# Joining six pairs of neighbouring loads in a two-layer decode kernel that streams all its data through one buffer

## The chip, the cores and the metric

The kernel runs on one core of a Trainium2 chip. The metric is the device time of one execution in microseconds (us); lower is better. A difference is spoken of as a share of the time of the kernel before.

## What is computed

Two layers of a decoder for one new token of four sequences (B = 4, D = 512). Each layer is an attention with a cache (32 query heads, 8 heads of keys and values, 4096 cached positions, 128 numbers each), and then a gated feed-forward network (F = 1792). Both layers use the same weights and the same cache. Everything is float32.

```python
x = A_x
x = x + A(_layernorm(x), k_cache, v_cache, wq, wo)
x = x + B(_layernorm(x), w1, w3, w2)
x = x + A(_layernorm(x), k_cache, v_cache, wq, wo)
x = x + B(_layernorm(x), w1, w3, w2)

# A: q = x @ wq; p = softmax(q k / sqrt(128)); (p @ v) @ wo
# B: (silu(x @ w1) * (x @ w3)) @ w2
```

## The kernel before

**One array, one buffer.** The host lays weights and cache side by side in one array `rows` of 128 partitions, in the order in which layer 0 uses them. On the chip there is one buffer, `space`, of 218 slots; a slot is 256 numbers in each of 128 partitions, 128 KB. All reading from memory is a list of loads, `LOADS`, one DMA each, written out by hand. An entry `(src, n, at)` copies n slots from slot `src` of the array into the buffer from slot `at` on. Two entries named "stash" are no DMAs but copies from PSUM by ScalarE.

**When a load is issued.** `pump` (line 120) goes through the list in its order and never past an entry whose slots are not all free:

```python
            if any(taken[at:at + n]):
                return
            taken[at:at + n] = [True] * n
            ...
                nc.sync.dma_start(place(at, n), rows[:, lo:lo + n * KB])
```

`done` (line 149) gives slots back after the last use in program order, and calls `pump`. So the list fixes where each DMA stands in the program. On the chip SyncE (SP) issues the DMAs (line 140) in this order; each first waits until the engine that last read its slots is through. The DMAs take eight semaphores in turn, and before a semaphore is used again SP waits for the load that used it last. The waits of SP stand in its queue: a load that waits holds up every load behind it.

**Who waits for a load.** A consumer waits for the whole DMA that holds its piece, since a DMA has one semaphore.

**Attention.** Keys and values of a head come as 32 tiles of 4 slots: tiles 0 to 15 are keys, 16 to 31 values, and each kind is in two halves of 8 tiles (the halves `c` of the cache). `score` (line 311, matmuls at L322) multiplies the query with 8 tiles of keys. `maximum`, `exponent` (ScalarE, L341) and `turn` (TensorE transposes at L348, and the VectorE copy at L350) make the weights. `weigh` (line 381, matmuls at L387) multiplies these with 8 tiles of values. For one head TensorE runs: score, turn, score, `weigh` of the first half, `turn` of the second half's weights, `weigh` of the second half. TensorE works through its queue in order.

**Where the layers meet.** Layer 0 takes the heads 0 to 7, layer 1 takes them from 7 down to 0, so that head 7 stays in the buffer. Its keys of tiles 0 and 1 must make room, though: they are copied into PSUM and brought back later (the stash). The last of these four copies is `store_last` (line 392): ScalarE copies half of tile 1 into the PSUM buffer of `turn`, once VectorE has copied the turned weights out of it (`finish`, line 398, calls `turn`, then `store_last`, then the second `weigh`). Only after it are the slots of tile 1 (158 to 162) free. The next load in the list, w3's first part `(1180, 16, 146)`, goes into slots 146 to 162, and so it waits for that copy at L395. Behind it in the list come w1 and the rest of w3 and w2, for the feed-forward of layer 0 (`feed_forward`, line 454: L463 for w1 and w3, L503 for w2), then the head 7 values that were given up, then head 6 for layer 1.

Of the kernel before, what the change touches and what calls it, by code (L numbers as in the profile page):

```python
# [52 lines left out]
    (0, 32, 186), (32, 64, 54), (96, 64, 118), (160, 64, 0), (224, 64, 91), (288, 64, 24), (352, 48, 88),  # L53
    (400, 48, 136), (448, 64, 28), (512, 60, 92), (572, 64, 152), (636, 52, 92), (688, 32, 144), (720, 40, 178),
    (1120, 32, 60), (760, 64, 113), (824, 40, 177), (864, 28, 92), (892, 36, 120), (928, 32, 174), (960, 32, 92),
    (992, 32, 154), (1024, 32, 186), (1056, 16, 0), (1072, 16, 92), (1088, 16, 108), (1104, 8, 124), (1112, 8, 132),
    (1180, 16, 146), (1152, 8, 0), (1160, 8, 8), (1168, 12, 16), (1196, 6, 140), (1202, 6, 146), (1208, 4, 158),
    (1212, 4, 152), (1216, 2, 156), (1218, 4, 140), (1222, 2, 144), (1224, 4, 146), (1228, 2, 150), (1230, 2, 158),
    (1232, 2, 160), (1234, 2, 152), (1056, 4, 154), (1060, 4, 140), (1064, 4, 144), (1068, 4, 148), (864, 4, 158),
    (868, 8, 68), (876, 4, 186), (880, 4, 190), (884, 8, 194), ("stash", 1, 202), (892, 8, 206), ("stash", 0, 214),  # L60
    (900, 8, 84), (908, 12, 162), (920, 12, 174), (932, 32, 108), (964, 20, 140), (984, 8, 36), (736, 28, 190),
    (764, 36, 84), (800, 64, 120), (608, 64, 52), (160, 32, 116), (672, 64, 154), (480, 64, 52), (544, 36, 148),
    (580, 28, 190), (320, 64, 28), (8, 24, 92), (384, 64, 154), (192, 64, 28), (256, 64, 140), (32, 32, 28),
    (64, 32, 60), (96, 32, 104), (128, 16, 136), (144, 8, 39), (152, 8, 28), (0, 8, 210), (1180, 16, 164),
    (1196, 12, 95), (1208, 8, 108), (1216, 8, 58), (1224, 4, 214), (1228, 4, 210), (1232, 2, 0), (1234, 2, 182),
)
# [580 lines left out]
```

## Time and profile before

| | us |
|---|---|
| median of 3 runs | 704.14 |
| lowest and highest | 703.93, 704.21 |
| the profiled execution, whole | 704.12 |
| its span, first to last instruction | 702.3 |
| TensorE busy in the span | 421.3 |
| VectorE busy | 144.5 |
| ScalarE busy | 41.7 |

The whole time is 1.8 us longer than the span; this lies ahead of the first instruction and behind the last. Views of the trace that are used below: the page of the profile (shares of engines and DMA queues, and the chain of waits that ended last), the chain by time (each step with start and length in us, a DMA from its issue to its landing), the timeline (start, length, engine, line, and in brackets the idle time ahead and what ended it), the DMA issues (KB, and us from issue to landing), and sums over stretches (busy time of each engine, granted TensorE clock, DMA share, GB/s). SPq is SyncE's queue; a count such as x16 in a matmul row takes in the weight loads, so it is 8 matmuls.

### The profile page before, as it was taken

Reading aid. Unit: us, or ns where it says so; the run is one execution under the profiler, and the core shown is the slowest. Engines: PE = TensorE matmul, PEld = TensorE weight load, DVE = VectorE, ACT = ScalarE, POOL = GpSimd, SP = SyncE. Lnnn points to the kernel's source line nnn. Section 1 sums busy time; section 2 is a strip of 40 time slices with the busy share of each in tenths; the row PEclk is TensorE's granted clock in tenths of the full one; section 3 lists DMA queues with packets and bytes.
Section 4 is the critical chain, followed back from the end, with each engine's and each line's share of the span. In section 5 each row is a group of like instructions: output and inputs, shape, how many; then the busy total and the mean of one; then the engine's idle time right before and its main releaser. Section 6 shows DMA issues by size and latency. Waiting matters only on the chain.

```text
span 702.3 us, 7502 instructions
## 1 busy us (share of the span) xinstructions
PE 421.3 (60%) x3280; PEld 133.4 (19%) x3280; DVE 144.5 (21%) x512; ACT 41.7 (6%) x100; POOL 3.1 (0%) x10
## 2 busy tenths in 40 slices
PE   1265466644578409667688985744555734567576
PEld 0111121201112103121124221201111211121223
DVE  2012112121023103330231322112120301213221
ACT  0010000100001001000101210000100001000100
POOL 0000000000000000000000000000000000000000
PEclk9997677876769859886999997877877958779999
DMA  9999999999999999999999999999999999999996
GB/s 422 418 415 425 467 419 418 426 457 417 449 414 444 424 438 415 436 423 427 422 418 378 423 430 440 439 438 418 441 440 414 450 419 448 430 425 417 424 425 268
DMA packets 12991, 297.87 MB, mean 424 GB/s; under 512 B 1440, under 2 KB 1568, under 8 KB 4512
## 3 DMA queue, kind: packets, MB, share of 16 engines
q1 hardware_dynamic: 12960, 297.41, 99.0%
q8 instruction: 25, 0.41, 0.2%
q14 instruction: 6, 0.05, 0.0%
HBM read 297.34 MB, written 0.07 MB: 423 GB/s over the span
## 4 chain that ended last, share of the span: by engine, by line
DMA 71%; PE 24%; DVE 1%; another core or an unknown queue 1%; ACT 1%; issue 1%; SPq 0%; ACTq 0%; DVEq 0%
DMA space<-in_rows 71%; PE o L387 10%; PE scores L322 9%; PE sums_ps L306 1%; PE turned L348 1%; ACT p L341 1%; PE scores L202 1%; PE stored L251 1%; DVE acc L335 0%; DVE pT L350 0%; PE o L463 0%; SPq L140 0%; PE sums_ps L431 0%; PE sums_ps L420 0%
## 5 line engine op out<-in xcount | busy, mean ns | idle before, releaser
L322 PE MATMUL scores<-space,qT 128*32 128x512 f32 x1024 | 170.0, 713 | 141.6 <-DMA space<-in_rows 140.8
L387 PE MATMUL o<-space,pT 128*16 128x512 f32 x1024 | 152.8, 710 | 99.3 <-DMA space<-in_rows 91.5
L322 PEld LDWEIGHTS scores<-space,qT 128*32 128x32 f32 x1024 | 36.0, 123 | 218.6 <-issue 180.0
L387 PEld LDWEIGHTS o<-space,pT 128*16 128x16 f32 x1024 | 31.7, 108 | 198.3 <-issue 94.2
L335 DVE TENSOR_REDUCE acc<-scores 128x1 f32<-128x512 f32 x32 | 22.1, 691 | 181.5 <-PE scores L322 181.5
L341 ACT ACTIVATE p<-scores,acc 128x512 f32<-128x512 f32 x30 | 20.6, 687 | 559.0 <-DVE acc L335 432.1
L410 DVE SCALAR_TENSOR_TENSOR o<-o,acc,o 128x128 f32<-128x128 f32 x112 | 39.3, 351 | 49.2 <-PE o L387 45.8
L350 DVE COPY pT<-turned 128x256 f32<-128x256 f32 x32 | 13.6, 425 | 154.3 <-PE turned L348 154.3
L348 PE MATMUL turned<-ident,p 128*128 128x128 f32 x128 | 21.9, 296 | 11.8 <-ACT p L341 11.8
L295 PE MATMUL sums_ps<-space,xT 128*32 128x512 f32 x120 | 22.9, 704 | 2.4 <-DMA space<-in_rows 2.4
L421 DVE COPY o<-sums_ps 128x16 f32<-128x16 f32 x16 | 2.8, 175 | 98.1 <-PE sums_ps L420 98.1
L348 PEld LDWEIGHTS turned<-ident,p 128*128 128x128 f32 x128 | 14.0, 145 | 44.1 <-ACT p L341 25.7
L306 PEld LDWEIGHTS sums_ps<-same,shares 128*128 128x128 f32 x120 | 16.3, 211 | 16.8 <-DVE shares L301 11.1
L306 PE MATMUL sums_ps<-same,shares 128*128 128x4 f32 x120 | 17.6, 270 | 0.9 <-DVE shares L301 0.9
L463 PE MATMUL o<-space,xT 128*32 128x192 f32 (+1 forms) x256 | 13.7, 355 | 3.2 <-DMA space<-in_rows 1.5
L441 PE MATMUL stored<-space,o 128*32 128x512 f32 x104 | 13.5, 592 | 0.0
L301 DVE TENSOR_SCALAR shares<-sums_ps,columns 128x512 f32<-128x512 f32 x15 | 11.1, 743 | 1.7 <-PE sums_ps L295 1.7
L503 PE MATMUL sums_ps<-space,hT 128*4 128x128 f32 x224 | 9.1, 272 | 3.6 <-DMA space<-in_rows 2.9
L211 PE MATMUL o<-columns,same 128*32 128x1 f32 x64 | 2.0, 181 | 14.3 <-DVE columns L548 13.3
L420 PEld LDWEIGHTS sums_ps<-columns,o 128*128 128x128 f32 x32 | 6.1, 239 | 20.6 <-issue 13.0
L463 PEld LDWEIGHTS o<-space,xT 128*32 128x32 f32 x256 | 7.6, 110 | 8.4 <-DVE h L480 2.8
L420 PE MATMUL sums_ps<-columns,o 128*128 128x16 f32 x32 | 7.7, 318 | 0.6 <-DVE o L410 0.6
(101 smaller groups left out, 141.9 us busy)
## 6 DMA issues: line engine op xcount, KB each, us to landing
space<-in_rows SPq DMA_DIRECT2D x11, 4096.0 KB, 21.6
space<-in_rows SPq DMA_DIRECT2D x14, 1024.0 KB, 18.6
space<-in_rows SPq DMA_DIRECT2D x3, 4608.0 KB, 24.6
space<-in_rows SPq DMA_DIRECT2D x2, 6144.0 KB, 30.9
space<-in_rows SPq DMA_DIRECT2D x6, 2048.0 KB, 29.2
space<-in_rows SPq DMA_DIRECT2D x3, 3584.0 KB, 23.5
space<-in_rows SPq DMA_DIRECT2D x2, 5120.0 KB, 28.7
space<-in_rows SPq DMA_DIRECT2D x1, 7680.0 KB, 33.8
```

The lines of the kernel that those rows point to most:

```text
L295: nc.tensor.matmul(wide[32 * k:32 * k + 32, :], xT[:, 32 * k:32 * k + 32], w[:, k, :], start=True, stop=True)
L306: nc.tensor.matmul(misc[:, h * B:(h + 1) * B], shares[:, h * DH:(h + 1) * DH], same[:, 0:B], start=True, stop=True)
L322: nc.tensor.matmul(ps[32 * b:32 * b + 32, :], qT[:, b, at:at + 32], t[:, i * BLOCK:(i + 1) * BLOCK], start=(m < 2), stop=(m >= TILES - 2))
L335: nc.vector.tensor_reduce(acc[:, i:i + 1], ps, axis=AX.X, op=ALU.max, negate=True)
L341: nc.scalar.activation(p.rearrange("p n s -> p (n s)"), ps, AF.Exp, bias=acc[:, i:i + 1], scale=1.0 if scale is None else scale, accum_out ...
L348: nc.tensor.transpose(pt[:, n, :], p[:, n, :], ident)
L350: nc.vector.tensor_copy(pT, pt.rearrange("p n (b r) -> p n b r", b=B)[:, :, :, 0:ROW])
L387: nc.tensor.matmul(o_ps[i][32 * b:32 * b + ROW, :], pT[:, r // 2, b, :], t[:, j * NB * DH:(j + 1) * NB * DH], start=(r < 2), stop=(r >= TI ...
L410: nc.vector.scalar_tensor_tensor(o, o_ps[s][:, j * DH:(j + 1) * DH], acc[:, 16 + NB * s + j:17 + NB * s + j], o, op0=ALU.mult, op1=ALU.add)
L420: nc.tensor.matmul(misc[:, 0:B * REP], o, head, start=True, stop=True)
L441: nc.tensor.matmul(bank[32 * h:32 * h + 32, :], oT[:, h, :], w[:, h, :], start=first, stop=last)
L463: nc.tensor.matmul(bank[32 * j:32 * j + 32, s], xT[:, 32 * k:32 * k + 32], w[:, j], start=(k == 0), stop=(k == KC - 1))
```

## The change

Six times two neighbouring entries of `LOADS` become one entry. Nothing else in the file is changed. The order of the list stays, and there are six DMAs fewer, of the same bytes.

| join | before | after | what it holds |
|---|---|---|---|
| 1 | (1072, 16, 92), (1088, 16, 108) | (1072, 32, 92) | layer 0, head 7: value tiles 20 to 23 and 24 to 27 |
| 2 | (1152, 8, 0), (1160, 8, 8) | (1152, 16, 0) | layer 0: first columns of w1, chunks 0, 1 and 2, 3 |
| 3 | (1230, 2, 158), (1232, 2, 160) | (1230, 4, 158) | layer 0: w2 chunks 11 and 12 |
| 4 | (876, 4, 186), (880, 4, 190) | (876, 8, 186) | layer 1, head 6: key tiles 3 and 4 |
| 5 | (908, 12, 162), (920, 12, 174) | (908, 24, 162) | layer 1, head 6: key tiles 11 to 13, and 14, 15 with value tile 16 |
| 6 | (544, 36, 148), (580, 28, 190) | (544, 64, 148) | layer 1, head 3: value tiles 16 to 24, and 25 to 31, which move from slots 190 to 218 into 184 to 212 |

```diff
...
-    (992, 32, 154), (1024, 32, 186), (1056, 16, 0), (1072, 16, 92), (1088, 16, 108), (1104, 8, 124), (1112, 8, 132),
+    (992, 32, 154), (1024, 32, 186), (1056, 16, 0), (1072, 32, 92), (1104, 8, 124), (1112, 8, 132),
...
```

The table is two lines shorter, so line numbers below it are smaller by 2 in the kernel after. SP's queue of the kernel before, from the load (1056, 16, 0) to w3's second part; 128x4096 is 16 slots or 2048 KB, DMAHW is the semaphore of an earlier load, PE and Activation are TensorE and ScalarE as last readers:

```order
L140 DMA space<-in_rows 128x4096
L140 DMA space<-in_rows 128x4096 [waits DMAHW4_49,PE_49]
L140 DMA space<-in_rows 128x4096 [waits PE_49]
L140 DMA space<-in_rows 128x2048 x2
L140 DMA space<-in_rows 128x4096 [waits DMAHW5_49,Activation_49]
L140 DMA space<-in_rows 128x2048 [waits DMAHW7_49,PE_49]
L140 DMA space<-in_rows 128x2048 [waits DMAHW6_49,PE_49]
L140 DMA space<-in_rows 128x3072
L140 DMA space<-in_rows 128x1536 [waits DMAHW0_49]
```

The same place after the change:

```order
L138 DMA space<-in_rows 128x4096
L138 DMA space<-in_rows 128x8192 [waits DMAHW4_49,PE_49]
L138 DMA space<-in_rows 128x2048 x2
L138 DMA space<-in_rows 128x4096 [waits DMAHW5_49,Activation_49]
L138 DMA space<-in_rows 128x4096 [waits DMAHW7_49,PE_49]
L138 DMA space<-in_rows 128x3072
L138 DMA space<-in_rows 128x1536 [waits DMAHW6_49]
```

Join 1 makes one 128x8192 of two 128x4096, join 2 one 128x4096 of two 128x2048. The load that waits for ScalarE (Activation) stands where it stood, two loads of 128x2048 behind join 1.

TensorE's queue of the kernel before, from the value tiles 20 to 23 of head 7 on (o_94 is the result of the first `weigh`, o_95 that of the second):

```order
L387 MATMUL o_94<-space,pT 16x512 [waits DMAHW0_49]
L387 MATMUL o_94<-space,pT 16x512 x7
L348 MATMUL turned<-ident,p 128x128 [waits Activation_49]
L348 MATMUL turned<-ident,p 128x128 x3
L387 MATMUL o_95<-space,pT 16x512 [waits DMAHW1_49,DVE_49]
L387 MATMUL o_95<-space,pT 16x512 x7
L387 MATMUL o_95<-space,pT 16x512 [waits DMAHW2_49]
```

After the change:

```order
L385 MATMUL o_94<-space,pT 16x512 [waits DMAHW0_49]
L385 MATMUL o_94<-space,pT 16x512 x7
L346 MATMUL turned<-ident,p 128x128 [waits Activation_49]
L346 MATMUL turned<-ident,p 128x128 x3
L385 MATMUL o_95<-space,pT 16x512 [waits DVE_49]
L385 MATMUL o_95<-space,pT 16x512 x7
L385 MATMUL o_95<-space,pT 16x512 [waits DMAHW1_49]
```

The order of the matmuls is the same. The first row now waits for the joined load, which stands ahead of the transposes; the first matmul of o_95 has no wait for a load any more.

More of the change, by code (lines that the diff above doesn't have):

```diff
@@ L55 @@
     (1120, 32, 60), (760, 64, 113), (824, 40, 177), (864, 28, 92), (892, 36, 120), (928, 32, 174), (960, 32, 92),
[4 rows of a table removed]
-    (868, 8, 68), (876, 4, 186), (880, 4, 190), (884, 8, 194), ("stash", 1, 202), (892, 8, 206), ("stash", 0, 214),
[3 rows of a table removed]
[3 rows of a table added]
+    (868, 8, 68), (876, 8, 186), (884, 8, 194), ("stash", 1, 202), (892, 8, 206), ("stash", 0, 214),
[2 rows of a table added]
     (64, 32, 60), (96, 32, 104), (128, 16, 136), (144, 8, 39), (152, 8, 28), (0, 8, 210), (1180, 16, 164),
```

10 rows, old and new, of the table LOADS are left out of this document.

## The prediction

> **What bounds the kernel now.** I read the page first: how full each engine and the DMA queue are, and which chain ended last.
>
> ```profile
> span 702.3 us, 7502 instructions
> DMA  9999999999999999999999999999999999999996
> q1 hardware_dynamic: 12960, 297.41, 99.0%
> DMA 71%; PE 24%; DVE 1%; another core or an unknown queue 1%; ACT 1%; issue 1%; SPq 0%; ACTq 0%; DVEq 0%
> ```
>
> The queue that carries the loads is busy for 99.0% of the span, and no slice but the last is under nine tenths. So the DMA engines are the bound, and hardly anything else counts: a change gains only by making the 297.41 MB cheaper to move, and loses whenever it lets the queue run dry, since nothing makes up for that later. The sums over three stretches show where bytes are dear.
>
> ```profile
> 40.00:340.00 300.00, 179.02 (x1186) 53.13 (x1186) 59.95 (x203) 14.96 (x40) 0.00 (x0) 0.78 1.00 430
> 340.00:400.00 60.00, 47.28 (x558) 18.71 (x559) 14.77 (x58) 9.94 (x21) 1.26 (x2) 0.94 1.01 406
> 400.00:690.00 290.00, 176.75 (x1317) 53.65 (x1316) 62.01 (x223) 15.09 (x38) 0.55 (x1) 0.81 1.00 431
> ```
>
> The last column is GB/s. Where the layers meet (340 to 400 us) it is 406 instead of 430, at a DMA share of 1.0: busy, but on smaller loads. At full rate these bytes would take 60 x 406 / 430.5 = 56.6 us, so 3.4 us are lost there. Some 31 loads land in it, so a load costs at most 3.4 / 31 = 0.11 us beyond its bytes.
>
> **What a load costs.** The chain by time gives landings to a hundredth.
>
> ```profile
> 364.62 10.62 DMA space<-in_rows
> ...
> 376.24 5.59 DMA space<-in_rows
> ```
> ```profile
> 472.69 23.07 DMA space<-in_rows
> ...
> 503.03 31.46 DMA space<-in_rows
> ```
>
> The lower two are landings at 495.76 and 534.49; by the list two loads of 64 slots (16.78 MB) came between them, in 38.73 us: 433.2 GB/s. The upper two are landings at 375.24 and 381.83; by the list eight loads of 2 or 4 slots with 2.62 MB came between, in 6.59 us. At 433.2 GB/s the bytes would take 6.05, so eight loads cost 0.54 us: 0.07 each. Six loads fewer gain 6 x 0.07 = **0.4 us**; by the stretch above 0.7 at most, and nothing at least. I take 0.4, from the row of the small loads themselves.
>
> In the Trainium skill, "DMA: Bandwidth & Descriptors", section "Anatomy of one DMA", a DMA has a fixed cost of about 2.0 us, and "Rules for kernel authors" there says to join many small transfers into one. If each of the six paid that on the path, the estimate would be 12 us, or 692; the rows above have 0.07 in place of 2.0, since in a full queue the next load moves while the last one completes.
>
> **What a joined load delays.** It can be issued only when both places are free, so its first half is issued later; and it lands once, so its first half is there later. The first costs something only if the queue ahead runs short. Here are the second loads of the pairs, in the order of the joins, each with its time from issue to landing:
>
> ```profile
> space<-in_rows SPq DMA_DIRECT2D x1, 2048.0 KB, 27.9
> ...
> space<-in_rows SPq DMA_DIRECT2D x1, 1024.0 KB, 13.8
> ...
> space<-in_rows SPq DMA_DIRECT2D x1, 256.0 KB, 5.5
> ...
> space<-in_rows SPq DMA_DIRECT2D x1, 512.0 KB, 7.5
> ...
> space<-in_rows SPq DMA_DIRECT2D x1, 1536.0 KB, 12.8
> ...
> space<-in_rows SPq DMA_DIRECT2D x1, 3584.0 KB, 28.3
> ```
>
> Their own bytes take 4.8, 2.4, 0.6, 1.2, 3.6 and 8.5 us at 433.2 GB/s; the rest, 4.9 us for join 3 and 6 to 23 for the others, is work queued ahead. So when each joined load is issued, at the time of its second half, the queue still has 4.9 us or more. An empty queue needs at most 2.4 us to move again (below). The later issue costs nothing at any of the six.
>
> The later landing holds up TensorE. For join 3 that is by 0.6 us at most, in front of a queue of 4.9 us: nothing. Joins 2, 4 and 5 had their second halves issued, and were first used, at these times:
>
> ```profile
> 351.49 0.38 SPq L140 DMA_DIRECT2D space<-in_rows  x1
> ...
> 386.05 0.38 SPq L140 DMA_DIRECT2D space<-in_rows  x1
> ...
> 395.75 0.33 SPq L140 DMA_DIRECT2D space<-in_rows  x1
> ```
> ```profile
> 365.17 1.07 PE L463 MATMUL o<-space,xT 128*32 128x256 f32 x16
> ...
> 404.55 1.90 PE L322 MATMUL scores<-space,qT 128*32 128x512 f32 x16
> ...
> 411.76 1.91 PE L322 MATMUL scores<-space,qT 128*32 128x512 f32 x12
> ```
>
> The second halves landed at 351.49 + 13.8 = 365.3, 386.05 + 7.5 = 393.6 and 395.75 + 12.8 = 408.6: 0.1 us after the first use for join 2, ahead of it for the others. Join 6 puts off the first `weigh` of head 3 by the 8.5 us of its second half at most; what waits for the end of that head is a load of 64 slots:
>
> ```profile
> 558.06 41.85 DMA space<-in_rows
> ```
>
> Issued 8.5 us later it would have 33 us to its landing, of which its own bytes take 19.4: nothing again. If these covers were thinner than the rows say, each would cost what join 1 does.
>
> **Join 1 is the costly one.** What stands on the way from its first half to the next load, in the timeline:
>
> ```profile
> 340.61 1.91 PE L387 MATMUL o<-space,pT 128*16 128x512 f32 x16 [0.86 <-DMA space<-in_rows]
> ...
> 345.50 3.39 PE L387 MATMUL o<-space,pT 128*16 128x512 f32 x16 [2.98 <-DMA space<-in_rows]
> ...
> 348.82 0.66 PE L348 MATMUL turned<-ident,p 128*128 128x128 f32 x4
> ...
> 349.51 0.42 DVE L350 COPY pT<-turned 128x256 f32<-128x256 f32 x1 [8.14 <-PE turned L348]
> ...
> 349.97 0.60 ACT L395 ACTIVATE turned<-space 128x512 f32<-128x512 f32 x1 [8.27 <-DVE pT L350]
> ...
> 350.51 1.91 PE L387 MATMUL o<-space,pT 128*16 128x512 f32 x16 [1.04 <-DVE rows L356]
> ...
> 350.60 1.85 SPq L140 DMA_DIRECT2D space<-in_rows  x4
> ```
>
> Tiles 20 to 23 land, TensorE starts on them at 345.50, transposes, VectorE copies, ScalarE makes its last stash copy, and at 350.60 SP issues w3's first part, 5.10 us after TensorE's start. That SP waited for this copy and nothing later:
>
> ```profile
> SPq L140 <- ACT turned L395: 24.6, 1, 24.6
> ```
>
> Behind it on SP all of w1, w3 and w2 are queued. Ahead of it in the DMA queue are the two 1024 KB loads behind join 1, and how long those last is in the chain by time; the waiting load's own row follows.
>
> ```profile
> 323.28 32.04 DMA space<-in_rows
> ```
> ```profile
> space<-in_rows SPq DMA_DIRECT2D x1, 2048.0 KB, 9.7
> ```
>
> The second of them lands at 355.32, and w3's part at 350.60 + 9.7 = 360.3, one load later: no pause, with 4.7 us in hand. After the change tiles 20 to 23 are there only when 24 to 27 are: issued at 322.44, 27.9 us to landing, so at 350.3 instead of 345.5. If all runs on as before, w3 is issued at 350.3 + 5.1 = 355.4, when the last load ahead of it has just landed. The queue is empty, and every load for the feed-forward stands behind this one.
>
> The 5.10 us depend on TensorE's clock. The 8 matmuls at 345.50 took 3.39 us, those at 350.51 took 1.91; the sums over these stretches have the clock in the column ahead of the DMA share.
>
> ```profile
> 345.50:348.40 2.90, 2.90 (x16) 0.48 (x16) 0.00 (x0) 0.00 (x0) 0.00 (x0) 0.50 0.93 393
> 348.60:351.80 3.20, 2.16 (x21) 0.83 (x20) 2.05 (x12) 1.81 (x2) 0.00 (x0) 1.00 1.04 422
> ```
>
> After 2.98 us of idling the clock was 0.50; after the change TensorE idles from 342.5 to 350.3, so I take 0.50 again. At full clock the issue would be 1.48 us earlier, at 353.9. At half clock for the transposes as well it would be 0.46 later, at 355.9; the price of these at half clock is in another place:
>
> ```profile
> 198.99 1.12 PE L348 MATMUL turned<-ident,p 128*128 128x128 f32 x4
> ```
>
> The Trainium skill, "TensorE: Matmul & The Clock Gate", Part 1, says that the clock falls to half after an idle window of about 3.4 us and needs a busy one of that length to rise; by it the half clock is certain here and may last through the transposes, which is the sum with 355.4 to 355.9.
>
> What an empty queue costs the trace shows only at its two ends: the first load, and the store of the output.
>
> ```profile
> space<-in_rows SPq DMA_DIRECT2D x1, 4160.0 KB, 12.2
> ...
> out<-space SPq DMA_DIRECT2D x1, 64.0 KB, 1.5
> ```
>
> The first: 4.26 MB take 9.8 us at 433.2 GB/s, so 2.4 us go to starting and landing. The second: 0.15 us of bytes, so 1.35. The first is the nearer, a load into an idle queue. w3's 2.10 MB take 4.8 us, so it lands at 355.4 + 2.4 + 4.8 = 362.6 instead of 360.3: **2.3 us late**. The ends: 2.8 (issue at 355.9), 1.3 (1.35 in place of 2.4), 0.8 (issue at 353.9) and 0 (both).
>
> TensorE's own delay I cost at nothing: it starts the second `weigh` some 0.6 us ahead of the new issue, at 354.8 in place of 350.51, but no longer waits within it for the two 1024 KB loads, which are there by then. So it comes out of the attention late by no more than some 2 to 4 us, and what it needs next, w3, is late by 2.3 too; the slots that it frees after that shift with the loads. If that cover is gone, the rest of these 4 us comes on top.
>
> **The sum.** Against the profiled execution's own 704.12 us, 0.02 under the median of the runs: -0.4 + 2.3 = +1.9, or **706.0 us**. From -0.7 (no pause) to +2.8 (nothing gained).
>
> **The rivals.**
>
> *The pause is short.* TensorE's clock comes back early, or a queue in the middle of the program starts faster than the first load did. Loss 0 to 1.3, net -0.4 to +0.9: about 704.4. For it: the store's 1.35. Against it: a TensorE that idles for 7.8 us.
>
> *No pause at all.* The w3 load is issued before 352.9, 2.4 us ahead of the end of the queue; the chain from landing to issue would have to take 2.6 us in place of 5.10. Then only the gain is left: 703.7, not slower. This is also what comes out if the joined half's landing isn't what the first `weigh` waits for. Against it speaks TensorE's queue, whose first row there waits for the joined load.
>
> *The short loads are the loss.* All 3.4 us lost between 340 and 400 go away with deeper loads, in spite of the pause: 704.12 - 3.4 + 2.3 = 703.0; faster. Against it: 25 of the 31 loads remain. If a load cost what the empty queue shows, 6 x 2.4 = 14 us would go and the time be 690; that the eight loads took 6.59 us speaks against it. This second one is the skill's fixed cost.
>
> *A second pause.* One of the later joins also drains the queue: 2 us more, 708.0. Against it: 4.9 us or more ahead of each.
>
> **How the numbers follow.** A measurement of this kernel can tell about 0.2%, 1.4 us, from no change. The forecast (pause of 1.3 to 2.8 us) has 0.66; of this 0.58 is beyond 1.4 us after the gain, 0.08 within. The short pause has 0.20 (same), no pause 0.07 (same), the dear loads 0.04 together (faster), the second pause 0.03 (slower). So faster 0.04, same 0.35, slower 0.61. The range takes in no pause and the longest pause with nothing gained, and a little beyond: 703.7 to 707.2.
>
> **What would show it.** In the trace after: w3's issue near 355.4 instead of 350.6, still behind ScalarE's copy (L393 there); the 1024 KB load ahead of it lands near 355.3; w3 lands about 7.2 us after its issue; a stretch between 355 and 358 with far fewer GB/s; everything behind late by some 2 us and no more. I am wrong if the issue is before 353, if GB/s shows no hole there, or if the later loads catch up.

## The result, and the profile after

The kernel after takes 708.19 us (median of 6 runs, 707.28 to 708.71) against 704.18 of the kernel before beside it (703.93 to 704.76): a ratio of 1.0055, with a 95% interval of 1.0042 to 1.0068. It is slower by 4.0 us. The forecast was 706.0, and its range ended at 707.2: the direction was right, the size half of what it is. The profiled execution took 707.70 us, 3.6 more than that of the kernel before.

The page of the kernel after, the same parts as were shown of before:

```profile
span 705.9 us, 7490 instructions
DMA  9999999999999999999989999999999999999996
q1 hardware_dynamic: 12096, 297.41, 98.4%
DMA 70%; PE 26%; DVE 2%; another core or an unknown queue 1%; ACT 1%; issue 1%; SPq 0%; ACTq 0%; DVEq 0%
```

There are fewer packets for the same 297.41 MB. The queue is busy for 98.4% of a longer span instead of 99.0%, and one slice, the 21st, has fallen from 9 to 8. The sums over the three stretches of the kernel after (the last columns are granted clock, DMA share and GB/s):

```profile
40.00:340.00 300.00, 178.28 (x1186) 53.15 (x1186) 59.96 (x203) 14.60 (x38) 0.00 (x0) 0.78 1.00 431
340.00:400.00 60.00, 41.30 (x525) 17.89 (x529) 13.12 (x51) 8.83 (x18) 1.25 (x2) 0.94 0.94 379
400.00:690.00 290.00, 180.26 (x1284) 52.40 (x1280) 62.97 (x229) 15.54 (x40) 0.11 (x1) 0.81 1.00 431
```

The outer two are as before. Where the layers meet, the DMA share is 0.94 instead of 1.01 and the rate 379 GB/s instead of 406. So the loss arose there. The timeline of the kernel after at that place:

```profile
340.63 1.91 PE L385 MATMUL o<-space,pT 128*16 128x512 f32 x16 [0.91 <-DMA space<-in_rows]
...
350.47 3.62 PE L385 MATMUL o<-space,pT 128*16 128x512 f32 x16 [7.93 <-DMA space<-in_rows]
354.02 0.66 PE L346 MATMUL turned<-ident,p 128*128 128x128 f32 x4
354.72 0.42 DVE L348 COPY pT<-turned 128x256 f32<-128x256 f32 x1 [13.37 <-PE turned L346]
...
355.17 0.60 ACT L393 ACTIVATE turned<-space 128x512 f32<-128x512 f32 x1 [13.50 <-DVE pT L348]
355.20 3.63 PE L385 MATMUL o<-space,pT 128*16 128x512 f32 x32 [0.52 <-DVE pT L348]
...
355.80 10.32 SPq L138 DMA_DIRECT2D space<-in_rows  x6
```

This is the chain that the prediction foresaw, step by step: TensorE idles 7.93 us for the joined load instead of 2.98, works at half clock on tiles 20 to 23, and ScalarE's last stash copy ends at 355.77 instead of 350.57. SP still waits for this copy last and issues w3 at 355.80 instead of 350.60:

```profile
SPq L138 <- ACT turned L393: 29.8, 1, 29.8
```

The DMA issues give from issue to landing, for w3's first load (issued at 355.80) and the joined w1 load behind it:

```profile
space<-in_rows SPq DMA_DIRECT2D x1, 2048.0 KB, 7.4
...
space<-in_rows SPq DMA_DIRECT2D x1, 2048.0 KB, 12.9
```

w3 lands at 363.2, 2.9 us later than the 360.3 of before. Now the sums over short stretches, first of the kernel after:

```profile
350.00:353.00 3.00, 2.53 (x12) 0.49 (x16) 0.00 (x0) 0.00 (x0) 0.00 (x0) 0.50 0.82 341
353.00:355.00 2.00, 1.68 (x12) 0.42 (x4) 0.28 (x1) 0.00 (x0) 0.00 (x0) 0.73 0.15 61
355.00:358.00 3.00, 2.80 (x28) 0.83 (x32) 2.69 (x14) 2.09 (x3) 0.00 (x0) 1.00 0.47 109
358.00:361.00 3.00, 2.42 (x14) 0.82 (x6) 1.61 (x6) 0.00 (x0) 0.00 (x0) 1.00 0.97 415
```

The hole is deeper than the late landing says, and it begins earlier. The last load ahead of w3 landed at 355.35, yet from 353 to 355 us the DMA share is already 0.15. The share is a mean over 16 DMA engines (a transfer's whole time counts where it starts). The trace records sixteen completions of each load. Of this last load, seven came from 352.01 to 352.86, seven more from 353.68 to 353.96, and the last two at 355.26 and 355.35: most engines were through well ahead of the landing, which is the last completion. The idle DMA time is 3 x 0.18 + 2 x 0.85 + 3 x 0.53 = 3.8 us. With the forecast gain of 0.4 us for six loads fewer, that is 3.4 us net, where the profiled executions differ by 3.6.

The same records show what the pause did to the engines' order. In the kernel before, the completions of w3's first load are spread from 357.35 to 360.25; in the kernel after, from 362.52 to 363.22. The last of them is 2.97 us late, but on the mean of the sixteen they are 4.4 us late.

So at this point there were two ways to count the loss. **Theory 1**, the prediction's: it is the lateness of w3, the pause of the last DMA engine (2.9 us here). **Theory 2**: it is the idle time of all 16 together (3.8 us), since the engines that were ahead lose their head start in the pause. Two rivals blame something else: **rival A**, that one of the other five joins costs about 1 us as well; **rival B**, that the size of the joined load costs, not its lateness.

### The profile page after: what moved, and what is told of

It reads as the page before. It is cut to its first block, busy times and chain, and to the rows that moved or that the text cites. A ratio compares the mean times of both kernels' runs of the same rounds, so it can differ in the third digit from the quotient of the medians.

```text
span 705.9 us, 7490 instructions
## 1 busy us (share of the span) xinstructions
PE 421.1 (60%) x3280; PEld 133.6 (19%) x3280; DVE 144.5 (20%) x512; ACT 41.7 (6%) x100; POOL 3.0 (0%) x10
## 3 DMA queue, kind: packets, MB, share of 16 engines
q1 hardware_dynamic: 12096, 297.41, 98.4%
## 4 chain that ended last, share of the span: by engine, by line
DMA 70%; PE 26%; DVE 2%; another core or an unknown queue 1%; ACT 1%; issue 1%; SPq 0%; ACTq 0%; DVEq 0%
DMA space<-in_rows 70%; PE scores L320 11%; PE o L385 8%; PE sums_ps L304 1%; PE turned L346 1%; ACT p L339 1%; DVE acc L333 1%; PE stored L249 1%; DVE o L408 0%; PE sums_ps L293 0%; PE o L461 0%; PE stored L439 0%; PE sums_ps L501 0%; DVE pT L348 0%
## 5 line engine op out<-in xcount | busy, mean ns | idle before, releaser
L385 PE MATMUL o<-space,pT 128*16 128x512 f32 x1024 | 149.3, 700 | 100.5 <-DMA space<-in_rows 93.2
L346 PE MATMUL turned<-ident,p 128*128 128x128 f32 x128 | 23.6, 313 | 11.3 <-ACT p L339 11.2
```

The lines of the kernel that those rows point to most:

```text
L346: nc.tensor.transpose(pt[:, n, :], p[:, n, :], ident)
L385: nc.tensor.matmul(o_ps[i][32 * b:32 * b + ROW, :], pT[:, r // 2, b, :], t[:, j * NB * DH:(j + 1) * NB * DH], start=(r < 2), stop=(r >= TI ...
```

## The experiments

For each, "350 to 358" is a row of sums of its profile; what its DMA share lacks to that of before, times 8 us, is the idle DMA time. The row of the kernel before, and that of the kernel after:

```profile
350.00:358.00 8.00, 5.59 (x33) 1.20 (x34) 3.20 (x15) 2.06 (x3) 0.00 (x0) 0.83 1.01 419
```
```profile
350.00:358.00 8.00, 7.01 (x48) 1.74 (x52) 2.97 (x14) 2.09 (x3) 0.00 (x0) 0.75 0.52 184
```

8 x (1.01 - 0.52) = 3.9 us by this coarser row. Intervals are those of the ratio to the kernel before, run beside each.

**Five joins without the first.** In the kernel after:

```diff
-    (1072, 32, 92),
+    (1072, 16, 92), (1088, 16, 108),
```

> Joins 2 to 6 alone, join 1 undone. Theory (all of the 4.0 us is join 1: it holds back the copy for which w3's load waits, and the DMA queue runs dry): 703.8 us, 0.35 under the kernel before (5 loads x 0.07 us), no hole in the queue between 355 and 358 us. Rival A (one of the later joins costs about 1 us as well): 705 us or more.

Measured: 703.96 us, ratio 0.9993 (0.9982 to 1.0003). The row of 350 to 358:

```profile
350.00:358.00 8.00, 5.09 (x35) 1.00 (x35) 3.95 (x16) 2.00 (x3) 0.00 (x0) 1.00 1.03 419
```

No hole, and no slower than the kernel before. Rival A falls. The gain of five loads fewer, 0.2 us, is within what can be told from nothing.

**Join 1 alone.** In the kernel before:

```diff
-    (1072, 16, 92), (1088, 16, 108),
+    (1072, 32, 92),
```

> Join 1 alone. Theory: 708.5 us, the kernel after plus five loads at 0.07 us; w3's first load is issued near 355.8 us and lands near 363.2. Rival A (a later join costs 1 us): 707.2 us or less.

Measured: 707.78 us, ratio 1.0050 (1.0037 to 1.0063): the whole loss within its interval. w3 is issued at 356.42 in its profile, 0.6 us later than forecast, mainly since here the four transposes ran at half clock too (1.11 us).

```profile
350.00:358.00 8.00, 6.84 (x32) 1.70 (x36) 2.38 (x13) 2.09 (x3) 0.00 (x0) 0.50 0.47 169
```

**The two halves apart, but in the other order.** In the kernel before:

```diff
-    (1072, 16, 92), (1088, 16, 108),
+    (1088, 16, 108), (1072, 16, 92),
```

> The kernel before with the two halves of join 1 left apart but loaded in the other order, so that value tiles 20 to 23 land second, at 350.4 us, as they do in the joined load; as many loads as before, of the same sizes. Theory (what counts is when these tiles are there): 708.5 us, w3 issued near 355.8. Rival B (the size of the joined load, or its single DMA, is what costs): 704.2 us.

Measured: 707.92 us, ratio 1.0050 (1.0038 to 1.0062). The timeline shows the same wait without any joined load, and the same half clock:

```profile
350.57 3.62 PE L387 MATMUL o<-space,pT 128*16 128x512 f32 x16 [7.89 <-DMA space<-in_rows]
...
355.52 0.60 ACT L395 ACTIVATE turned<-space 128x512 f32<-128x512 f32 x1 [13.71 <-DVE pT L350]
...
356.14 0.80 SPq L140 DMA_DIRECT2D space<-in_rows  x2
```
```profile
350.00:358.00 8.00, 6.92 (x44) 1.87 (x48) 2.66 (x13) 2.09 (x3) 0.00 (x0) 0.71 0.48 175
```

Rival B falls: what costs is when tiles 20 to 23 are there, not how many DMAs bring them.

**All six joins, with work put ahead of the wait.** In the kernel after, w3's first load is cut; chunks 0 to 2 need no slot of tile 1:

```diff
-    (1180, 16, 146),
+    (1180, 12, 146), (1192, 4, 158),
```

> All six joins, but w3's first load cut in two: chunks 0 to 2 (1536 KB, slots 146 to 158), which need not wait for the last stash copy, and chunk 3 (512 KB, slots 158 to 162), which does. Theory: the first part is in the queue early and gives it 3.6 us of work beyond 355.3, the second is issued near 355.8 with some 3 us in hand, so there is no pause: 703.8 to 704.2 us. Rival A: 705 us. If TensorE's own delay of 1.5 to 4 us at this place costs time by itself: 705.5 us or more.

Measured: 705.33 us, ratio 1.0028 (1.0009 to 1.0046). Its row:

```profile
350.00:358.00 8.00, 6.96 (x44) 1.93 (x48) 2.50 (x13) 2.09 (x3) 0.00 (x0) 0.66 0.87 344
```

This missed: by the medians more than half of the loss is gone, but 1.2 us are left, though the queue had 3.6 us more to do and w3's last part landed at 360.4, hardly later than before. The single executions range from 704.03 to 710.98, four of the twelve at 707.98 or more, so the interval is wide (0.6 to 3.2 us). Theory 1 has no place for the 1.2 us; the DMA share does: 8 x (1.01 - 0.87) = 1.1 us. It could also have been TensorE's own delay; the last two runs below bear on that.

**A smaller delay.** In the kernel before the same bytes are cut elsewhere, so that tiles 20 to 23 are only 2.5 us late:

```diff
-    (1072, 16, 92), (1088, 16, 108),
+    (1072, 24, 92), (1096, 8, 116),
```

> The kernel before with the same 4096 KB cut at another place: value tiles 20 to 25 in one load, 26 and 27 in a second; as many loads as before. Tiles 20 to 23 land 2.5 us late instead of 4.9, w3's load is issued near 353.2 us. Theory 1 (what is lost is the pause of the last DMA engine to finish, as the prediction had it): 0.3 us, so 704.5 us. Theory 2 (what is lost is the idle time of all 16 DMA engines together, most of which finish some 3 us before the last): the mean DMA share falls short by 1.2 to 1.5 us between 350 and 358, so 705.4 us.

Measured: 705.13 us, ratio 1.0011 (1.0002 to 1.0020). w3 was issued at 353.68, before the last load ahead of it had landed.

```profile
350.00:358.00 8.00, 7.48 (x40) 1.76 (x36) 3.06 (x14) 2.09 (x3) 0.00 (x0) 0.56 0.76 292
```

1.0 us over the kernel before by the medians, 0.8 by the ratio (0.1 to 1.4). This run doesn't tell the theories apart: the interval shuts neither out, and w3 was issued later than the forecast took it to be and landed at 361.12, 0.9 us late, which would fit theory 1 as well. The idle DMA time of the row, 2.0 us, is more than was lost.

**TensorE kept busy while it waits.** In the kernel after, in `weigh`, ahead of tile 20; the extra matmuls add nothing to the result:

```diff
         for r in range(TILES):
+            if (layer, g, i, r) == (0, TURN, 0, 4):
+                for _ in range(7):
+                    busy(4)
```

> The kernel after with seven extra matmuls of 128x512 on TensorE while it waits for the joined load (their result is not used), so that its clock stays at full speed. Theory 1 and 2: the matmuls on tiles 20 to 23 take 1.9 us instead of 3.6, w3 is issued near 354.1 instead of 355.8. Theory 1: 705.1 us. Theory 2: 706.0 to 706.5 us. If the clock has no part in the loss: 708.2.

Measured: 706.66 us, ratio 1.0039 (1.0025 to 1.0054): under the kernel after by 1.5 us by the medians, by 1.1 by the ratios, whose intervals overlap. The timeline, and the row of sums:

```profile
350.37 1.91 PE L388 MATMUL o<-space,pT 128*16 128x512 f32 x16
...
353.36 0.60 ACT L396 ACTIVATE turned<-space 128x512 f32<-128x512 f32 x1 [11.94 <-DVE pT L348]
...
353.99 0.80 SPq L138 DMA_DIRECT2D space<-in_rows  x2
```
```profile
350.00:358.00 8.00, 7.48 (x56) 1.90 (x54) 3.91 (x17) 2.09 (x3) 0.00 (x0) 1.00 0.71 272
```

The clock is 1.00, the same eight matmuls take 1.91 us instead of 3.62, and w3 is issued 1.8 us earlier. So the half clock was some 1.1 to 1.5 us of the loss. What is left of it is 2.6 us by the medians, and 1.9 in the profiled execution; the idle DMA time, 2.4 us, less 0.4 for the joins, is 2.0. w3's landing, at 361.2, is only 1.0 us late: theory 1 had 705.1, under the whole interval (705.9 to 707.9).

**What a load costs.** In the kernel before each of the 16 loads of 64 slots is cut into four; the first of them:

```diff
-    (0, 32, 186), (32, 64, 54),
+    (0, 32, 186), (32, 16, 54), (48, 16, 70), (64, 16, 86), (80, 16, 102),
```

> The kernel before with each of its 16 loads of 64 slots cut into four of 16: 48 loads more, the same bytes in the same order and places. It prices a load where nothing else changes. At 0.07 us a load, as predicted: 3.4 us more, 707.5. At 0.11, the bound of the prediction: 709.4. If a load costs nothing beyond its bytes: 704.2. With a fixed 2 us each: 800.

Measured: 707.82 us, ratio 1.0052 (1.0040 to 1.0064). That is 3.7 us for 48 loads, 0.078 us each. The prediction's 0.07 stands; neither nothing nor 2 us.

**Still more work ahead of the wait.** As in the run with the cut, and the joined w1 load also goes ahead of w3's chunk 3:

```diff
-    (1180, 16, 146), (1152, 16, 0),
+    (1180, 12, 146), (1152, 16, 0), (1192, 4, 158),
```

> All six joins; w3's first load cut as in the run before (chunks 0 to 2 ahead of the last stash copy), and the joined w1 load also put ahead of chunk 3, so that the DMA queue has 8.5 us of work beyond 355.3 us. Theory 2: no engine runs dry, DMA share stays near 1.0 from 350 to 370, 703.8 us; the 1.2 us that was left with the cut alone goes. Rival (the 1.2 us is TensorE's own delay, not idle DMA engines): 705.3 us.

Measured: 704.40 us, ratio 1.0009 (0.9996 to 1.0023), with single executions up to 709.6. Its profile is of that slowest one and so can't speak for the median. It has no hole here,

```profile
350.00:358.00 8.00, 7.07 (x32) 1.69 (x36) 2.61 (x13) 2.09 (x3) 0.00 (x0) 0.50 1.03 435
358.00:400.00 42.00, 34.98 (x473) 16.47 (x469) 9.31 (x34) 5.68 (x12) 1.25 (x2) 0.94 0.94 352
```

but one behind it: a share of 0.94 from 358 to 400 us, 42 x 0.07 = 2.9 us. The median speaks for theory 2, though its interval overlaps that of the run with the cut alone. The slow execution has a second pause, but at 5.5 us over the kernel before, the pause is only about half of what it lost; the rest is not explained.

**The joined load kept, and the wait taken away.** In the kernel after, w3's first load goes four slots lower and touches no slot of tile 1:

```diff
-    (1180, 16, 146),
+    (1180, 16, 142),
```

> All six joins, and w3's first load four slots lower (142 to 158 instead of 146 to 162), so that it needs none of tile 1's slots and waits for no copy that TensorE's wait holds back; the price is that w3's second part (slots 140 to 146) is issued only when chunk 0 of w3 has been used, some 11 us later than before. TensorE still waits for the joined load. Theory 2: no DMA engine runs dry from 350 to 358 us, and the queue has enough for the later issue: 703.8 us, 0.4 under the kernel before. If TensorE's delay by the joined load costs by itself: 705.3 or more. If the later issue of w3's second part drains the queue: 705 to 706, with a hole after 365 us.

Measured: 704.19 us, ratio 1.0019 (0.9999 to 1.0040).

```profile
350.00:358.00 8.00, 7.07 (x44) 1.91 (x48) 2.61 (x13) 2.09 (x3) 0.00 (x0) 0.67 1.03 434
```

No hole at 350 to 358, and the median is 4.0 us under the kernel after with all six joins in it. TensorE waits for the joined load as before, so by the median its delay costs nothing that can be measured once the DMA engines have work. The forecast 703.8 was not reached, and a few executions are longer, up to 712.4; these raise the ratio, which leaves anything up to 2.8 us open. Why they are longer was not tried.

**The two theories on the traces.** The profiled executions can be laid side by side without the spread of the runs. All columns are in us against the profiled execution of the kernel before. Idle DMA time is counted transfer by transfer from 340 to 400 us, as a mean of the 16 engines; the fourth column is the mean of the sixteen completions of the kernel's last load.

| run | w3's first chunks land later | idle DMA time | last load completes later, on the mean | execution longer |
|---|---|---|---|---|
| five joins without the first | -0.1 | -0.1 | -0.3 | -0.6 |
| w3 moved (the run above) | 0.0 | 0.5 | 0.3 | 0.1 |
| w3 cut (chunk 3) | 0.1 | 1.1 | 1.0 | 1.0 |
| smaller delay | 0.9 | 1.8 | 1.4 | 1.2 |
| TensorE kept busy | 1.0 | 2.4 | 2.1 | 1.9 |
| the kernel after | 3.0 | 3.9 | 3.5 | 3.6 |
| other order | 3.1 | 4.2 | 3.7 | 4.4 |
| join 1 alone | 3.4 | 4.5 | 4.0 | 3.5 |

The mean completion of the last load follows the idle time in every row, 0.1 to 0.5 us short of it, with joins and without. The lateness of w3 misses it by up to 1.1 us, most plainly with w3 cut and with TensorE kept busy. From 400 to 690 us the idle time differs by some 0.1 us at most between these executions, so TensorE's delay made no further pause there. The last column adds how far the last engine trails at the very end, which varies by about 1 us. Left out are the run that cuts each long load into four, which has more loads, and the long execution of the run with still more work ahead: that one lost 2.9 us to idle engines, and its last load completed 4.3 us later.

No version beat the kernel before by more than can be measured; five joins without the first is level with it.

## Why the prediction was right in kind and wrong in size

**The bound, and what a load costs** (-0.4): right. The quarters gave 0.078 us a load, so six are worth 0.47 us. The rivals in which small loads or a fixed price of a DMA are the loss fall with it. So does, as a price on the path, the 2 us of the Trainium skill ("DMA: Bandwidth & Descriptors", "Anatomy of one DMA"), which that section gives for DMAs issued by GpSimd, while these are issued by SP: in a full queue a DMA paid 0.078. In an empty one w3 paid 7.4 - 4.8 = 2.6 us.

**Joins 2 to 6 cost nothing**: right, by the run with these five alone. "A second pause" in the kernel after falls too.

**Join 1 holds back the copy, the copy holds back w3, and the queue runs dry**: right, each step at its time. Issue 355.4 to 355.9 was forecast, 355.80 measured; it is the first weigh that waits, with one load or with two in the other order. The half clock was chosen rightly: 3.62 us for the eight matmuls, and full clock took 1.1 to 1.5 us off the time. The transposes ran at full clock in the kernel after (0.66 us) and at half clock with join 1 alone (1.11 us), the two cases that the forecast reckoned with. Less idling than the 3.4 us that the prediction goes by was enough for the half clock: 2.98 us in the kernel before, and 2.55 us with the five joins alone (clock 0.50 from 346.2 to 348.3 us).

**TensorE's own delay at nothing**: right, as far as the traces show. It made the DMA engines idle through the late copy; beyond that no idle time came of it.

**What an empty queue costs**: forecast 2.4 us to start again, measured 2.6; with the later issue w3 was 2.9 us late instead of 2.3. That is 0.6 us of the miss.

**The step that failed** is the next: "so it lands at 355.4 + 2.4 + 4.8 = 362.6 instead of 360.3: 2.3 us late", taken as the loss itself. A landing is that of the last of 16 DMA engines. The others had been ahead of it, and in a full queue they went on to the next load: in the kernel before, the completions of w3's first load are spread over 2.9 us. In the pause all stopped, and then started level: in the kernel after, over 0.7 us. The 350 to 353 row, 0.82, shows engines stopping while two loads were still under way. So the term is not 2.3 to 2.9 but the mean idle time, 3.8 to 3.9 us. The cut w3 load showed the difference by itself: there w3's last part was hardly late, and about 1.1 us were lost by the engines that were ahead. The 4.7 us "in hand" of the kernel before were reckoned to the landing at 355.32, but the first engine completed that load at 351.99, only 1.4 us after w3's issue. The rival without a pause reckons alike, with an issue before 352.9 as early enough; that is too late by the same head start of some 3 us.

That the head start exists could have been read in the trace of before. This row is the end of that kernel:

```profile
690.00:700.00 10.00, 6.84 (x153) 3.75 (x149) 1.70 (x7) 0.00 (x0) 0.00 (x0) 1.00 0.63 251
```

All loads had been issued by 686.7, the last landed at 699.03, and still the share over these 10 us is 0.63: 3.7 us idle on the mean, of which only 1.0 is behind the last landing. The other 2.7 us are engines that were done before the last one.

By the end of the kernel after, the engines are as far apart again (the last load completes from 698.32 to 702.49 us) as in the kernel before (694.56 to 699.03). What makes them drift apart, and why the idle time of those ahead comes back in full at the end although the last one sets the time, was not tried.

## What to carry to other kernels

In this kernel, which the DMA queue bounds, joining two loads saves under a tenth of a microsecond, and delays the first half by up to the length of the second; ask whose wait that lengthens, and whether a load stands behind that wait. What counts is how much is queued at the moment the waiting load is issued, on the DMA engine that is furthest ahead, not when the last landing comes: read the DMA share in stretches of 2 or 3 us, and cost a hole by its area. The join can stay if the next load needs nothing that the joined one holds back; here that brought the median back to the time before, and no lower.

## What was not expected of the hardware

The 16 DMA engines of one queue are not in step: with two loads under way, which landed at 352.90 and 355.35, the DMA share of 350 to 353 us was 0.82 and that of 353 to 355 was 0.15, and the completions of the later load lay 3.3 us apart. An interval in which TensorE waited 7.93 us put its clock at 0.50 for the next 3.6 us of work, which moved a DMA's issue by 1.8 us and the kernel's time by 1.1 to 1.5, in a kernel in which TensorE is busy for 60% of the span.
